# A transformer block on one Trainium2 core: the second query blocks' LayerNorm tiles turned by DMA in 16-bit halves, with three smaller moves

## The chip, the core and the metric

The kernel runs on one core of a Trainium2 chip. The core has a matrix engine (TensorE, in the profile PE, with its weight loads as PEld) and three engines for elementwise work: VectorE (DVE), ScalarE (ACT) and GpSimd (POOL). The fifth, SyncE (SP), issues nearly all DMA transfers, one after the other. Each engine works through its own instructions in order, and semaphores between the engines hold an instruction until its operands are there. TensorE writes into PSUM, of which a bank holds 128 x 512 numbers of 32 bits; everything else works from SBUF.

The metric is the device time of one execution in microseconds (us). The change is small against the whole, so differences of a few us matter, and times are given with one or two decimals.

## The reference

One block of a transformer with modulated LayerNorm: attention over the last 512 keys of a cache, then a gated feed-forward network (FFN). Cut to what matters:

```python
mod = (silu(c) @ w_mod).reshape(1, 6, 1, 512)
sa, ca, ga, sb, cb, gb = (mod[:, j] for j in range(6))
h = layernorm(x) * (1 + ca) + sa                  # x is 2048 x 512
q = (h @ wq)                                      # 32 heads of 128
p = softmax(q @ k.T * 128 ** -0.5)                # 512 keys, 8 key heads
x = x + ga * ((p @ v) @ wo)
h = layernorm(x) * (1 + cb) + sb
x = x + gb * ((gelu(h @ w_gate) * (h @ w_up)) @ w_down)     # 1792 wide
```

## The kernel before, in words

**Products in 16-bit halves.** TensorE is fed with 16-bit operands. A 32-bit number is held as two fp16 parts, a high part (a copy to fp16) and a low part (the number less its high part), and a product is made of three matmuls (`mm3`, lines 85 to 88: low x high, high x low, high x high). The first layers' products, x times wq and x times w_gate and w_up, go by a Strassen-like scheme with seven products of blocks instead of eight. Its blocks are called b11, b21, y, b22 and, for sums and differences of them, t1 to t4. They are cut from the normalised, modulated and transposed input: b11 and b21 from the first 512 queries of a half, y and b22 from the second 512.

**Stages.** The 2048 queries are worked in two halves of 1024, and each half in two query blocks (`qb`) of four tiles of 128 rows. LayerNorm therefore comes in four generations of eight tiles: generations 0 and 1 for the attention of the two halves, generations 2 and 3 for the FFN of the two halves. Attention runs as 512 steps `t`, one for each score tile (128 queries x 512 keys); a step has three score matmuls and in most steps nine others. The FFN runs as 28 sets `q` of seven products each, named (q, k); sets 0 to 13 serve the first half, 14 to 27 the second. A set has 42 matmuls, and beside the products go the output tiles `py` (`y_tasks`, six matmuls each, eight tiles for every two sets), which `y_next` places, four in a set.

**What sets the order.** In the attention part every engine's order is written out by hand: work is hung on step numbers with `at(...)`, `sched(...)` and `put_off(...)` and issued step by step, and the loads for a step wait in a list until a slot of their pool comes free. From FFN set 2 on, the program's order is fixed only for SP, while a planner that ships with the language orders TensorE, VectorE, ScalarE and GpSimd by its own estimate of when operands are ready. SP's order is the program's all the way through.

**The parts that the change touches:**

- `ln_tile` (lines 465 to 526) is the LayerNorm of a tile of generations 1 to 3: load, statistics (`ln_stat`, `ln_power`), normalisation (`norm`), four TensorE transposes of 128 x 128 in 32 bits into one PSUM bank (`turn`, line 495), the scaling by 1 + cb and shift by sb (`affine`, line 503, four ScalarE instructions of 128 x 128), and the store of the 256 KB tile to memory (`spill`, line 507). Generation 1 normalises on VectorE (line 490), generations 2 and 3 on ScalarE (lines 489 and 487). For generation 2, the tile `acc`, GpSimd makes the negative mean times the inverse deviation, `nmean` (line 482). Generation 3, the tile `xs`, finds its statistics ready, made by `ln_last` when attention ended.
- `attn_final` (line 920) hangs the seven parts of a generation 2 tile on the steps after a query tile's attention is finished: the statistics one step later, the normalisation six, the turn eight.
- Lines 1539 to 1544 hang the parts of the generation 3 tiles on products: tile i has q = 7 (2 + i // 2) + 3 (i % 2), loads at q - 4, is normalised at q + 2, turned at q + 4 and scaled at q + 5 and q + 6.
- `combos` (line 528) loads the stored blocks of a half again, makes the differences on GpSimd and their 16-bit parts on ScalarE and GpSimd (lines 363, 367 and 540). For generation 3 its two rounds start at the products numbered 49 and 63.
- The modulation rows are sums over 512 products for each output (`mod_col`, line 135: a VectorE multiply that also adds up, from a loaded tile `wmc`). Rows 3 and 4 are sb and cb. Four sums of each stand at steps 211 to 229; `mod_max` follows at 232 and `mod_scale` at 234, which turns the two maxima through TensorE and rescales both rows.
- In the profile `p<-ee,rr,p` (line 971) is the low part of the softmax, `qt` and `ot` (line 706) the low parts of queries and attention outputs, `pt<-p` (line 975) the DMA transpose of the softmax's two 16-bit halves, and `at` (line 1263) the low part of the FFN's inner result.

Of the kernel before, what the change touches and what calls it, by code (L numbers as in the profile page):

```python
# [63 lines left out]
def block_kernel(ctx: ExitStack, tc: tile.TileContext, x, kT, v, wq, wo, wg, wu, wd, cT, wc, wm, out):  # L64
# [8 lines left out]
    def tmp(name):  # L73
        return pool.tile([P, 512], F32, tag="e", name=name, bufs=NE)

    def raw(name):
        return pool.tile([P, 512], F32, tag="raw", name=name, bufs=NRAW)
# [14 lines left out]
    def dma(out_, in_):  # L92
        moved[0] += 1
        nc.sync.dma_start(out_, in_)
# [81 lines left out]
    def col(name, i=0):  # L176
        return ST[name][:, i:i + 1]
# [20 lines left out]
    def mod_max(j):  # L198
        m = little("mm", 2, 1)
        absmax(m, cols[:, j:j + 2, :])  # L200
        return m
# [34 lines left out]
    def pool_ts(out, src, a, b=1.0, op0=ALU.mult, op1=ALU.mult):  # L236
        nc.gpsimd.tensor_scalar(out, src, a, b, op0=op0, op1=op1)
# [108 lines left out]
    def spilled(gen, key):  # L346
        if (gen, key) not in hs:
            n = KT if key in (0, 1) else 2
            hs[gen, key] = dram.tile([P, n, QB], F32, name=f"hs{gen}_{key}")
        return hs[gen, key]  # L350
# [94 lines left out]
    def put_off(n, fn):  # L445

        waits_.append([n, fn])
# [17 lines left out]
    def ln_tile(gen, i, src):  # L465
        jsc, jsh = ln_cols("a" if gen < 2 else "f")
        qb, i = divmod(i % (2 * QT), QT)
        st = {}

        def load():  # L470
            if gen == 2:
                st["x"] = src()
            else:
                st["x"] = raw("xs")
                dma(st["x"], src())

        def stat():
            ln_stat(st["x"], st)
            ln_power(st)
            if gen == 2:  # L480
                st["nm"] = small.tile([P, 1], F32, name="nmean")
                pool_ts(st["nm"], st["mv"][:, 0:1], st["rs"], -1.0)

        def norm():
            if gen == 3:
                rs, nm = col("kmax", qb * QT + i), col("kinv", qb * QT + i)
                return nc.scalar.activation(st["x"], st["x"], AF.Identity, bias=nm, scale=rs)
            if gen == 2:
                return nc.scalar.activation(st["x"], st["x"], AF.Identity, bias=st["nm"], scale=st["rs"])
            nc.vector.tensor_scalar(st["x"], st["x"], st["mv"][:, 0:1], st["rs"], op0=ALU.subtract, op1=ALU.mult)  # L490

        def turn():
            st["ps"] = bank("acc", "pln", NACC)
            for dt in range(KT):
                nc.tensor.transpose(st["ps"][:, dt * P:(dt + 1) * P], st["x"][:, dt * P:(dt + 1) * P], ident)

        def affine(dts):
            if 0 in dts:
                st["f"] = raw("hf") if gen == 2 else tmp("hf")
            f = st["f"]  # L500
            for dt in dts:
                sl = slice(dt * P, (dt + 1) * P)
                nc.scalar.activation(f[:, sl], st["ps"][:, sl], AF.Identity,
                                     scale=cols[:, jsc, dt:dt + 1], bias=cols[:, jsh, dt:dt + 1])
            if KT - 1 in dts:
                def spill():
                    dma(spilled(gen, qb)[:, :, i * P:(i + 1) * P], f.rearrange("p (k q) -> p k q", k=KT))

                if gen == 3:
                    put_off(3, spill)  # L510
                else:
                    spill()

        def parts(act):
            o = slice(i * P, (i + 1) * P)
            f = st["f"].rearrange("p (k q) -> p k q", k=KT)
            for h, name in enumerate(("b11", "b21") if qb == 0 else (None, "b22")):
                if name:
                    t, src = block(gen, name), f[:, 2 * h:2 * h + 2, :]
                    if act:  # L520
                        nc.scalar.activation(t[:, 0:2, o], src, AF.Copy)
                    else:
                        nc.gpsimd.tensor_tensor(t[:, 2:4, o], src, t[:, 0:2, o], op=ALU.subtract)

        more = [lambda: parts(True), lambda: parts(False)] if gen < 3 else []
        return load, [nop if gen == 3 else stat, norm, turn, lambda: affine((0, 1)), lambda: affine((2, 3))] + more

    def combos(gen, p, eng, base=True, d=0, e=0):
        X = {}
# [167 lines left out]
    def at(key, *fns):  # L697
        later.setdefault(key, []).extend(fns)
# [425 lines left out]
    for dt in range(KT):  # L1124
        sched(6 + dt, (lambda dt=dt: gate_load(dt), [lambda dt=dt: gate_cols(dt)]), ahead=8)
    at(("d", 10), lambda: ts(cols[:, 2, :], gps["ps"][:, 0:KT], 1.0, None, ALU.mult))
    for j, ts_ in ((3, (211, 215, 223, 227)), (4, (213, 217, 225, 229)), (5, (274, 278, 282, 286))):
        for dt in range(KT):
            box = {}
            sched(ts_[dt], (lambda box=box, j=j, dt=dt: box.update(f=mod_load(j, dt)), [lambda box=box: box["f"]()]))  # L1130
    at(11, lambda: mod_row(2))
    mx = {}
    at(("w", 232), lambda: mx.update(m=mod_max(3)))
    at(234, lambda: mod_scale(3, "mf", 1.0, mx["m"]))

    def sched_combos(gen, p, base):
        for k, (load, steps) in enumerate(combos(gen, p, nc.gpsimd if gen or p == 0 else nc.vector, False, 0 if gen else 1 if p else 2, 0 if gen or p else 5)):
# [391 lines left out]
    def f_at(q, k, *fns):  # L1529
        at(("f", q, k), *fns)  # L1530
# [4 lines left out]
    for q in range(3, NQ):  # L1535
        for k, at_ in ((0, 2), (3, 2), (1, 3), (2, 4)):
            f_at(q - 1, at_, lambda q=q, k=k: set_fetch(("f", q), ("f", q % (2 * NP)), k))

    for i in range(2 * QT):
        load, steps = ln_tile(3, i, lambda i=i: y1[2 * QT + i])  # L1540
        q = 7 * (2 + i // 2) + 3 * (i % 2)
        f_at((q - 4) // 7, (q - 4) % 7, load)
        for k, fn in zip((0, 2, 4, 5, 6), steps):
            f_at((q + k) // 7, (q + k) % 7, fn)
    for p in range(2):
        q = 7 * (7 + 2 * p)
        for load, steps in combos(3, p, nc.gpsimd):
            f_at((q - 2) // 7, (q - 2) % 7, load)
            for off, fn in steps:
                f_at((q + 2 * off) // 7, (q + 2 * off) % 7, fn)  # L1550

    def f_final(ti):
        if ti >= 2 * QT:
# [6 lines left out]
    for q in range(NQ):  # L1560
        n, m = divmod(q, 2)
        its = items(NG + q) if q < 2 else f_items(q)
        for k, pk in enumerate(ORDER):
            if (q, pk) not in f_done:
                all_of(its[pk])
            run(("f", q, k))
            tick()
            if k in (1, 2, 5, 6):
                y_next()
        if m == 1:  # L1570
            for qi, (a, b) in enumerate((("11", "21"), ("12", "22"))):
                for i in range(QT):
                    nexty.append(y_tasks((2 * (n // NP) + qi) * QT + i, [lambda n=n, a=a: A[n, a], lambda n=n, b=b: A[n, b]],
                                         [("f", n, 0), ("f", n, 1)], col("dysc", n % NP), f_final if n % NP == NP - 1 else None))
# [39 lines left out]
```

## Time and profile before

| what | value |
|---|---|
| median of 3 runs | 1772.27 us (1769.34 to 1772.45) |
| the profiled execution | 1769.1 us, span 1767.3 us |
| TensorE's granted clock | 1.000 |
| TensorE / VectorE / ScalarE / GpSimd busy | 1730.0 / 1447.2 / 1219.3 / 882.2 us |
| attention's steps 0 to 511 | 26 to 1334 us of the span |
| sets 14 to 27 (second half of the FFN) | from about 1549 us |
| q1, the queue of SP's transfers | 325.44 MB, 80.0% of 16 DMA engines' span |

All times inside the kernel count from the start of the span. A row of a group has the engine, the operation, the tile written and the tiles read (`pln<-ident,xs`), partitions x elements and type, how often, and durations. Matmuls overlap: a matmul of 512 columns is shown with 0.38 us, but the next one starts 0.22 us after it, so the difference of two starts is what it costs TensorE. In a row of time order the first number is the start, the second the length, and a bracket at the end the idle time before it with what ended it. A row of waits has the waiting engine and its line, the engine and line waited for, the total, the count and the longest. A row of stretches has start and end, length, and busy time with the number of instructions in brackets for each engine, then the clock, the share of the DMA engines, and GB/s.

### The profile page before, as it was taken

Reading aid. Unit: us, or ns where it says so; the run is one execution under the profiler, and the core shown is the slowest. Engines: PE = TensorE matmul, PEld = TensorE weight load, DVE = VectorE, ACT = ScalarE, POOL = GpSimd, SP = SyncE. Lnnn points to the kernel's source line nnn. Section 1 sums busy time; section 2 is a strip of 40 time slices with the busy share of each in tenths; the row PEclk is TensorE's granted clock in tenths of the full one; section 3 lists DMA queues with packets and bytes.
Section 4 is the critical chain, followed back from the end, with each engine's and each line's share of the span. In section 5 each row is a group of like instructions: output and inputs, shape, how many; then the busy total and the mean of one; then the engine's idle time right before and its main releaser. Section 6 shows DMA issues by size and latency. Waiting matters only on the chain.

```text
span 1767.3 us, 25992 instructions
## 1 busy us (share of the span) xinstructions
PE 1730.0 (98%) x8114; PEld 796.3 (45%) x8114; DVE 1447.2 (82%) x2501; ACT 1219.3 (69%) x2830; POOL 882.2 (50%) x1119
## 2 busy tenths in 40 slices
PE   7899999999999999999999999999999999999998
PEld 4444444444444444444444444444444444444443
DVE  7888888888888998888888888888886768767676
ACT  5887787878778777897777777777674555434342
POOL 4879878776788873444565555555520024000000
PEclk9999999999999999999999999999999999999999
DMA  7999999989999997999999999999985643252222
GB/s 230 209 195 210 218 217 200 223 204 221 216 216 227 224 201 145 208 205 234 208 208 208 212 214 204 206 211 214 188 185 131 199 129 114 83 173 90 86 75 75
DMA packets 662122, 327.62 MB, mean 185 GB/s; under 512 B 553056, under 2 KB 575840, under 8 KB 661984
## 3 DMA queue, kind: packets, MB, share of 16 engines
q1 hardware_dynamic: 661696, 325.44, 80.0%
q8 instruction: 64, 1.05, 0.3%
q14 instruction: 74, 0.61, 0.1%
q10 hardware_dynamic: 288, 0.52, 0.1%
HBM read 131.73 MB, written 59.90 MB: 108 GB/s over the span
## 4 chain that ended last, share of the span: by engine, by line
PE 72%; DVE 14%; ACT 8%; issue 3%; POOL 2%; DMA 1%; SPq 0%; ACTq 0%; POOLq 0%; DVEq 0%
PE py L86 7%; PE py L88 7%; PE py L87 7%; DVE p L971 5%; PE ps L86 4%; PE ps L88 4%; PE ps L87 4%; PE po L86 4%; PE po L88 4%; PE po L87 4%; DVE nm L945 3%; PE fa L86 3%; PE fa L88 3%; PE fa L87 3%; ACT ee L954 2%
## 5 line engine op out<-in xcount | busy, mean ns | idle before, releaser
L954 ACT ACTIVATE ee<-ps,nm 128x512 f32<-128x512 f32 x512 | 350.9, 685 | 251.0 <-DVE nm L945 245.6
L971 DVE SCALAR_TENSOR_TENSOR p<-ee,rr,p 128x512 f16<-128x512 f32 x512 | 470.0, 918 | 0.9 <-ACT p L966 0.7
L945 DVE TENSOR_REDUCE nm<-ps 128x1 f32<-128x512 f32 x512 | 349.4, 683 | 77.0 <-PE ps L88 75.5
L966 ACT ACTIVATE p<-ee,rr 128x512 f16<-128x512 f32 x512 | 365.4, 714 | 2.3 <-DMA pt<-p 1.9
L86 PE MATMUL ps<-k,qt 128*128 128x512 f16 x512 | 194.1, 379 | 16.6 <-DVE qt L706 15.4
L86 PE MATMUL py<-wo,ot 128*128 128x512 f16 x512 | 194.1, 379 | 4.4 <-DVE ot L706 4.4
L87 PE MATMUL po<-pt,v 128*128 128x512 f16 x512 | 194.0, 379 | 0.0
L88 PE MATMUL po<-pt,v 128*128 128x512 f16 x512 | 194.0, 379 | 0.0
L87 PE MATMUL py<-wo,ot 128*128 128x512 f16 x512 | 194.0, 379 | 0.0
L88 PE MATMUL py<-wo,ot 128*128 128x512 f16 x512 | 194.0, 379 | 0.0
L86 PE MATMUL po<-pt,v 128*128 128x512 f16 x512 | 194.0, 379 | 0.0
L88 PE MATMUL ps<-k,qt 128*128 128x512 f16 x512 | 194.0, 379 | 0.0
L87 PE MATMUL ps<-k,qt 128*128 128x512 f16 x512 | 193.9, 379 | 0.0
L962 DVE RECIPROCAL rr<-rr 128x2 f32<-128x2 f32 x256 | 41.4, 162 | 99.6 <-ACT rr L959 98.5
L87 PEld LDWEIGHTS <-w 128*128 128x128 f16 x728 | 71.2, 98 | 86.2 <-issue 1.2
L88 PEld LDWEIGHTS <-w 128*128 128x128 f16 x728 | 71.2, 98 | 86.0 <-issue 0.2
L86 PEld LDWEIGHTS <-w 128*128 128x128 f16 x728 | 71.2, 98 | 85.5 <-DVE w L1016 0.3
L914 DVE SCALAR_TENSOR_TENSOR acc<-py,dysc,acc 128x512 f32<-128x512 f32 x112 | 81.6, 747 | 31.5 <-PE py L88 30.5
L954 ACT ACTIVATION_READ_ACCUMULATOR ee<-ps,nm 128x1 f32 x512 | 100.8, 197 | 0.0
L914 DVE SCALAR_TENSOR_TENSOR acc<-py,ysc,acc 128x512 f32<-128x512 f32 x128 | 94.7, 740 | 3.9 <-PE py L88 3.9
L706 DVE SCALAR_TENSOR_TENSOR ot<-po,ot 128x512 f16<-128x512 f32 x128 | 87.0, 680 | 0.0
L86 PE MATMUL py<-wo,at 128*128 128x512 f16 x224 | 84.9, 379 | 1.4 <-DVE at L1263 1.4
(270 smaller groups left out, 3765.9 us busy)
## 6 DMA issues: line engine op xcount, KB each, us to landing
w<-kept SPq DMA_DIRECT2D x123, 256.0 KB, 3.2
wo<-kept SPq DMA_DIRECT2D x60, 256.0 KB, 3.5
raw<-in_wo SPq DMA_DIRECT2D x56, 256.0 KB, 3.1
kept<-stage SPq DMA_DIRECT2D x56, 256.0 KB, 3.3
kept<-w SPq DMA_DIRECT2D x39, 256.0 KB, 3.4
rw<-in_wq SPq DMA_DIRECT2D x38, 256.0 KB, 3.3
hs<-hf SPq DMA_DIRECT2D x32, 256.0 KB, 2.7
pt<-p SPq DMA_TRANSPOSE x512, 3.5
```

The source lines that it names most:

```text
L86: nc.tensor.matmul(ps, llo, rhi, start=first, stop=False, skip_group_check=chain)
L87: nc.tensor.matmul(ps, lhi, rlo, start=False, stop=False, skip_group_check=chain)
L88: nc.tensor.matmul(ps, lhi, rhi, start=False, stop=last, skip_group_check=chain)
L706: return lambda: nc.vector.scalar_tensor_tensor(t[:, 1, :], src, scale, t[:, 0, :], op0=ALU.mult, op1=ALU.subtract)
L914: nc.vector.scalar_tensor_tensor(acc[ti], st["p"], by, acc[ti], op0=ALU.mult, op1=ALU.add)
L945: nc.vector.tensor_reduce(nm, E[t]["ps"], axis=AX.X, op=ALU.max, negate=True)
L954: nc.scalar.activation(e, E[t]["ps"], AF.Exp, bias=E[t]["nm"], scale=1.0, accum_out=sm[:, t % 2:t % 2 + 1])
L962: return lambda: nc.vector.reciprocal(r, r)
L966: nc.scalar.activation(p16[:, 0, :], E[t]["e"], AF.Copy, scale=E[t]["r"])
L971: nc.vector.scalar_tensor_tensor(p16[:, 1, :], E[t]["e"], E[t]["r"], p16[:, 0, :], op0=ALU.mult, op1=ALU.subtract)
```

## The change

Four things change, all in when and on which engine something is done; what is computed stays.

1. Generation 3 (the second half's input to the FFN) has a function of its own, `ln_turned`. A tile is loaded and normalised on ScalarE as before, then split into an fp16 copy (ScalarE) and its remainder (GpSimd), and both halves are turned by one DMA transpose from SP into a tile of the tag `pt`. When all four tiles of a query block are there, `turned_out` scales and shifts a whole 128 x 512 part: the high half on ScalarE, and the low half, scaled and added, on VectorE; it is stored three products later. A tile is now normalised at product q, split at q + 1 and turned at q + 3. The parts come out at products 31, 33, 35, 37 and 43 to 46, and the two rounds of `combos` start at 51 and 65.
2. Generation 2 is normalised on GpSimd, by one instruction with the mean and the inverse deviation, and `nmean` is no longer made.
3. The sums of rows 3 and 4 move from steps 211 to 229 to steps 243 to 257, `mod_max` to 258 and `mod_scale` to 260.
4. In the last set `y_next` is called after two products instead of four, so two output tiles more are left for the end.

```diff
@@ ln_tile
         def stat():
             ln_stat(st["x"], st)
             ln_power(st)
+
+        def norm():
             if gen == 2:
-                st["nm"] = small.tile([P, 1], F32, name="nmean")
-                pool_ts(st["nm"], st["mv"][:, 0:1], st["rs"], -1.0)
-
-        def norm():
-            if gen == 3:
-                rs, nm = col("kmax", qb * QT + i), col("kinv", qb * QT + i)
-                return nc.scalar.activation(st["x"], st["x"], AF.Identity, bias=nm, scale=rs)
-            if gen == 2:
-                return nc.scalar.activation(st["x"], st["x"], AF.Identity, bias=st["nm"], scale=st["rs"])
+                return pool_ts(st["x"], st["x"], st["mv"][:, 0:1], st["rs"], ALU.subtract, ALU.mult)
             nc.vector.tensor_scalar(st["x"], st["x"], st["mv"][:, 0:1], st["rs"], op0=ALU.subtract, op1=ALU.mult)
...
+    def ln_turned(i):
+
+        qb, i_ = divmod(i, QT)
+        st = {}
+
+        def load():
+            st["x"] = raw("xs")
+            dma(st["x"], y1[2 * QT + i])
+
+        def norm():
+            nc.scalar.activation(st["x"], st["x"], AF.Identity, bias=col("kinv", i), scale=col("kmax", i))
+
+        def split():
+            st["p"] = t = pool.tile([P, 2, W], F16, tag="p16", name="xh", bufs=NP16)
+            nc.scalar.activation(t[:, 0, :], st["x"], AF.Copy)
+            nc.gpsimd.tensor_tensor(t[:, 1, :], st["x"], t[:, 0, :], op=ALU.subtract)
+
+        def turn():
+            if i_ == 0:
+                TURN[qb] = pool.tile([P, QT, 2 * KT, P], F16, tag="pt", name="xt", bufs=NPT)
+            nc.sync.dma_start_transpose(TURN[qb][:, i_], st["p"].rearrange("p a b -> p (a b)"))
+
+        return load, norm, split, turn
+
+    def turned_out(qb, dt):
+        f = tmp("hf")
+        v = f.rearrange("p (t q) -> p t q", t=QT)
+        sc = cols[:, 4, dt:dt + 1]
+        nc.scalar.activation(v, TURN[qb][:, :, dt, :], AF.Identity, scale=sc, bias=cols[:, 3, dt:dt + 1])
+        nc.vector.scalar_tensor_tensor(v, TURN[qb][:, :, KT + dt, :], sc, v, op0=ALU.mult, op1=ALU.add)
+        put_off(3, lambda: dma(spilled(3, qb)[:, dt, :], f))
...
-    for j, ts_ in ((3, (211, 215, 223, 227)), (4, (213, 217, 225, 229)), (5, (274, 278, 282, 286))):
+    for j, ts_ in ((3, (243, 247, 251, 255)), (4, (245, 249, 253, 257)), (5, (274, 278, 282, 286))):
...
-    at(("w", 232), lambda: mx.update(m=mod_max(3)))
-    at(234, lambda: mod_scale(3, "mf", 1.0, mx["m"]))
+    at(("w", 258), lambda: mx.update(m=mod_max(3)))
+    at(260, lambda: mod_scale(3, "mf", 1.0, mx["m"]))
...
     for i in range(2 * QT):
-        load, steps = ln_tile(3, i, lambda i=i: y1[2 * QT + i])
         q = 7 * (2 + i // 2) + 3 * (i % 2)
-        f_at((q - 4) // 7, (q - 4) % 7, load)
-        for k, fn in zip((0, 2, 4, 5, 6), steps):
-            f_at((q + k) // 7, (q + k) % 7, fn)
+        load, norm, split, turn = ln_turned(i)
+        step(q - 4, load)
+        step(q, norm)
+        step(q + 1, split)
+        step(q + 3, turn)
+    for k, (qb, dt) in enumerate(((0, 0), (0, 2), (0, 1), (0, 3), (1, 0), (1, 2), (1, 1), (1, 3))):
+        step(31 + 2 * k if k < 4 else 39 + k, lambda qb=qb, dt=dt: turned_out(qb, dt))
     for p in range(2):
-        q = 7 * (7 + 2 * p)
+        q = 51 + 14 * p
...
-            if k in (1, 2, 5, 6):
+            if k in ((1, 2, 5, 6) if q < NQ - 1 else (1, 5)):
                 y_next()
```

More of the change, by code (lines that the diff above doesn't have):

```diff
@@ L505, in affine @@
             if KT - 1 in dts:
[L506 to L512, printed above, removed]
+                dma(spilled(gen, qb)[:, :, i * P:(i + 1) * P], f.rearrange("p (k q) -> p k q", k=KT))
         def parts(act):
@@ L523, in parts @@
                         nc.gpsimd.tensor_tensor(t[:, 2:4, o], src, t[:, 0:2, o], op=ALU.subtract)
-        more = [lambda: parts(True), lambda: parts(False)] if gen < 3 else []
-        return load, [nop if gen == 3 else stat, norm, turn, lambda: affine((0, 1)), lambda: affine((2, 3))] + more
+        more = [lambda: parts(True), lambda: parts(False)]
+        return load, [stat, norm, turn, lambda: affine((0, 1)), lambda: affine((2, 3))] + more
+    TURN = {}
+    def ln_turned(i):
[22 more added lines that the diff above has]
+        put_off(3, lambda: dma(spilled(3, qb)[:, dt, :], f))
     def combos(gen, p, eng, base=True, d=0, e=0):
@@ L1537, in block_kernel, with step @@
             f_at(q - 1, at_, lambda q=q, k=k: set_fetch(("f", q), ("f", q % (2 * NP)), k))
+    def step(q, fn):
+        f_at(q // 7, q % 7, fn)
     for i in range(2 * QT):
-        load, steps = ln_tile(3, i, lambda i=i: y1[2 * QT + i])
         q = 7 * (2 + i // 2) + 3 * (i % 2)
-        f_at((q - 4) // 7, (q - 4) % 7, load)
-        for k, fn in zip((0, 2, 4, 5, 6), steps):
-            f_at((q + k) // 7, (q + k) % 7, fn)
+        load, norm, split, turn = ln_turned(i)
[5 more added lines that the diff above has]
+        step(31 + 2 * k if k < 4 else 39 + k, lambda qb=qb, dt=dt: turned_out(qb, dt))
     for p in range(2):
-        q = 7 * (7 + 2 * p)
+        q = 51 + 14 * p
         for load, steps in combos(3, p, nc.gpsimd):
-            f_at((q - 2) // 7, (q - 2) % 7, load)
+            step(q - 2, load)
             for off, fn in steps:
-                f_at((q + 2 * off) // 7, (q + 2 * off) % 7, fn)
+                step(q + 2 * off, fn)
     def f_final(ti):
```

## The prediction

> **What bounds the kernel now.** I read the page first, then TensorE's waits, then stretches of the span.
>
> ```profile
> span 1767.3 us, 25992 instructions
> ...
> PE 1730.0 (98%) x8114; PEld 796.3 (45%) x8114; DVE 1447.2 (82%) x2501; ACT 1219.3 (69%) x2830; POOL 882.2 (50%) x1119
> ...
> PE 72%; DVE 14%; ACT 8%; issue 3%; POOL 2%; DMA 1%; SPq 0%; ACTq 0%; POOLq 0%; DVEq 0%
> ```
>
> TensorE (PE) is busy 98% of the span and is 72% of the chain that ended last. So a change counts only where it takes instructions from PE or closes one of its gaps. Its waits name the gaps:
>
> ```profile
> PE ps L86 <- DVE qt L706: 15.4, 12, 2.7
> ...
> PE py L86 <- DVE ot L706: 4.4, 4, 1.7
> ...
> PE pln L495 <- ACT hf L503: 1.5, 2, 0.8
> PE py L86 <- DVE at L1263: 1.4, 1, 1.4
> ```
>
> Each is total, count, longest. Most is PE waiting for VectorE (DVE). The stretches that the change touches, busy microseconds by engine:
>
> ```profile
> core 0: us, PE busy (x) PEld busy (x) DVE busy (x) ACT busy (x) POOL busy (x), PEclk, DMA share, GB/s
> 525.00:565.00 40.00, 39.40 (x187) 17.84 (x186) 34.76 (x59) 32.55 (x79) 34.30 (x43) 1.00 0.92 212
> 565.00:635.00 70.00, 66.13 (x307) 29.39 (x305) 65.90 (x125) 49.02 (x120) 59.62 (x71) 1.00 0.95 218
> 650.00:690.00 40.00, 38.25 (x179) 17.18 (x177) 33.47 (x55) 28.52 (x68) 20.44 (x22) 1.00 0.80 154
> 690.00:800.00 110.00, 107.46 (x515) 50.65 (x514) 93.61 (x177) 93.27 (x229) 47.00 (x63) 1.00 0.90 197
> 1375.00:1450.00 75.00, 75.00 (x365) 36.21 (x364) 50.16 (x77) 43.82 (x84) 2.80 (x8) 1.00 0.53 165
> 1450.00:1550.00 100.00, 100.00 (x465) 45.32 (x464) 75.71 (x109) 47.57 (x78) 27.89 (x21) 1.00 0.30 100
> ```
>
> From 1375 to 1550, where the second query blocks' LayerNorm tiles are now turned, PE never rests while ACT, DVE and GpSimd (POOL) do: work leaving PE there is gained whole. From 565 to 635, where eight modulation sums run, PE loses 3.87 and DVE is 94% busy. From 690 to 800, where the first blocks are normalised, PE loses 2.54.
>
> **Part A, the turns.** One turn as PE sees it:
>
> ```profile
> L495 PE MATMUL pln<-ident,xs x32: 272/273/273, 1385.3 to 1435.4; 128*128 128x128 f32 x32
> ```
>
> ```profile
> 1385.13 0.38 PE L88 MATMUL fc<-t,w 128*128 128x512 f16 x1
> 1385.35 0.60 PE L495 MATMUL pln<-ident,xs 128*128 128x128 f32 x4
> 1385.78 0.38 PE L86 MATMUL fa<-b,w 128*128 128x512 f16 x1
> ```
>
> The next product starts 0.43 us after the first of four transposes; the 273 ns are length, not pace. Eight tiles: 8 x 0.43 = 3.4 us leave a PE that has no gap. What comes instead, by the nearest rows (copies to 16 bit, their remainders, DMA transposes, a DVE multiply-add):
>
> ```profile
> L363 ACT ACTIVATE t<-cb x8: 614/629/631, 1452.1 to 1485.7; 128x512 f16<-128x512 f32 x8
> L367 POOL TENSOR_TENSOR t<-cb,t x8: 1151/1598/1613, 1454.6 to 1487.2; 128x512 f16<-128x512 f32 x8
> ```
>
> ```profile
> L975 SPq DMA_TRANSPOSE pt<-p x16: 1231/1232/1318, 656.5 to 692.7; - x16
> ```
>
> ```profile
> pt<-p SPq DMA_TRANSPOSE x512, 3.5
> ```
>
> ```profile
> 601.41 1.62 DVE L135 SCALAR_TENSOR_TENSOR wmc<-wmc,sbc 128x512 f32<-128x512 f32 x1
> ...
> 603.63 1.65 DVE L971 SCALAR_TENSOR_TENSOR p<-ee,rr,p 128x512 f16<-128x512 f32 x1
> ...
> 618.59 0.68 DVE L135 SCALAR_TENSOR_TENSOR wmc<-wmc,sbc 128x512 f32<-128x512 f32 x1
> ```
>
> ACT keeps eight normalisations, loses 32 quarter-size scalings, gains eight copies (0.63) and eight full-size scalings; POOL gains 8 x 1.6 = 12.8; DVE 8 x 0.68 = 5.4 (8 x 1.62 = 13.0 beside POOL); loads and stores stay eight of 256 KB each. All of it lies under PE: of the 175 us, DVE is idle 49, ACT 84, POOL 144. I take nothing; without that cover the DVE part alone would cost 5.4. The chain's end moves by two steps: the last remainder starts at 1487.2, and the second half's first products start here:
>
> ```profile
> 1549.85 0.38 PE L86 MATMUL fa<-b,w 128*128 128x512 f16 x1
> ```
>
> That leaves about 61 us; a set has 66 matmuls at 0.216 us, so two steps of its seven are some 4 us. The new wait is on SP, whose order is the program's: eight transposes of 1.23 us stand there behind POOL's remainder, and behind them the next tiles' loads and the next sets' weights. Before, the tile's store waited there in the same way:
>
> ```profile
> SPq L94 <- ACT hf L503: 18.4, 2, 16.5
> ```
>
> ```profile
> 1407.30 0.58 SPq L94 DMA_DIRECT2D w<-kept  x1
> ```
>
> ```profile
> w<-kept SPq DMA_DIRECT2D x31, 256.0 KB, 3.5
> ```
>
> ```profile
> 1411.70 0.38 PE L86 MATMUL fa<-b,w 128*128 128x512 f16 x1
> ```
>
> One store held SP 16.5 us and PE still did not wait; the tightest fetch I find lands at 1410.8 and is used 0.9 us later. The new chain skips PE's turn, so SP should wait less: nothing, with up to 8 x 2.6 (below) as the other end. Part A: -3.4, between -3.4 and +17.
>
> The Trainium skill speaks against this part: "VectorE: DVE Perf Modes", section "Rules for kernel authors", would give a 128x128 transpose to TensorE wherever a PSUM result will do, and its section "The three transpose paths" has 390 ns there against 1309 ns by DMA. By its figures, an estimate, 64 half-tiles by DMA are 84 us against 12.5 for 32 on TensorE. Were none of it hidden, part A would lose some 70 us by the page, where the rows give -3.4. The trace differs on both figures: 0.11 us of pace here, and 3.5 us for eight half-tiles by DMA.
>
> **Part B, the sums for the shift and scale of the second LayerNorm** move from steps 211-229 to 243-257, their scaling from 234 to 260: from the stretch 565-635 to 650-695. A step has three score matmuls, and counted in order those of step 243 begin here:
>
> ```profile
> 650.93 0.38 PE L86 MATMUL ps<-k,qt 128*128 128x512 f16 x1
> ```
>
> ```profile
> 565.00:635.00 70.00, 8.66 (x16) 1.00 0.95 218
> ```
>
> ```profile
> DVE nm L945 <- PE ps L88: 5.4, 7, 1.2
> ```
>
> ```profile
> L971 DVE SCALAR_TENSOR_TENSOR p<-ee,rr,p x17: 731/741/1257, 655.3 to 694.5; 128x512 f16<-128x512 f32 x17
> ```
>
> The sums take 8.66 of DVE in the old place (first row). The 40 us before them, like work without sums, lose 0.60, so 70 us would lose 1.05: the gain is 3.87 - 1.05 = 2.8. In the new place POOL is half idle, so I price a sum at 0.68 and its read-out 0.08, together 8 x 0.76 = 6.1, against 6.5 of idle DVE, 5.4 of which is DVE waiting for PE (second row, 655 to 695). What doesn't fit is 6.1 - 5.4 = 0.7. The eight loads leave a stretch with DMA share 0.95 for one with 0.80. Part B: -2.1, between -3.9 (all of the old gap goes) and +3.3 (all 6.1 is lost, 2.8 gained).
>
> **Part C, the first blocks' normalisation goes from ACT to POOL.**
>
> ```profile
> 741.06 0.81 ACT L489 ACTIVATE acc<-acc,nmean,rs 128x512 f32<-128x512 f32 x1
> 741.76 0.68 ACT L954 ACTIVATE ee<-ps,nm 128x512 f32<-128x512 f32 x1
> ...
> 743.61 0.81 ACT L503 ACTIVATE hf<-pln,cols 128x128 f32<-128x128 f32 x2
> ```
>
> ```profile
> 744.48 0.66 PE L495 MATMUL pln<-ident,acc 128*128 128x128 f32 x4 [0.79 <-ACT hf L503]
> ```
>
> ```profile
> L237 POOL TENSOR_SCALAR gs<-gate,osc x8: 683/692/1123, 68.9 to 588.4; 128x512 f32<-128x512 f32 x8
> ```
>
> A turn waits until ACT has read the bank before it; ACT spent 0.7 us just ahead (741.06 to 741.76) on the normalisation. Two such waits make the 1.5 of the list: without it both shrink by 0.7, -1.4. POOL pays 8 x 0.69 and drops eight small products; it is busy 47 of 110, and the normalisation comes two steps of twelve matmuls, some 5 us, ahead of its turn. Ends: -2.5 (all idle time of the stretch) and +6.7: beside POOL the DVE row of p took 1.65 where 0.74 is its median in the quiet stretch, some 0.84 more for each of eight. I take -1.4, since the wait is seen and DVE has 16 us to spare.
>
> **Part D, two of the last pair's output tiles wait for the end.**
>
> ```profile
> 1755.58 0.39 PE L86 MATMUL py<-wo,at 128*128 128x512 f16 x1 [1.39 <-DVE at L1263]
> ```
>
> At the end PE has nothing ready for 1.39 us. Two tiles of six matmuls (2.6 us) now lie there: -1.4. Their two accumulations could push DVE's last halves by 2 x 0.68, so the end on the other side is 0.
>
> **Sum.** -3.4 - 2.1 - 1.4 - 1.4 = -8.3. The profiled execution took 1769.1, 1.8 more than its span; the median of the runs, 1772.27, lies 3.2 above it. From the median: 1764.0; from the profiled execution 1760.8.
>
> **Rivals.** *The gaps only move* (0.20). B and C give nothing, since DVE stays at nine tenths and some other step waits: 1772.3 - 3.4 - 1.4 = 1767.5. For it: DVE holds most of PE's waits; against it: its 5.4 idle us in the new place.
>
> *The sums crowd DVE* (0.12). B costs its 3.3, C nothing: 1772.3 - 3.4 + 3.3 - 1.4 = 1770.8. For it: a gap of 1.75 stands in 650-690 already. The rows of one DVE instruction at 0.68 and 1.62 are what decides.
> The Trainium skill's "SBUF — State Buffer", section "SBUF: two separate sides", says why: DVE with two SBUF inputs and POOL lock one port pair, and the later blocks. The trace agrees (0.68 against 1.62).
>
> *SP's queue starves PE* (0.10), the slower side. Each transpose holds SP for copy, remainder and issue, 0.63 + 1.60 + 1.23 = 3.5; less the 0.9 of slack, weights could come 2.6 late, eight times: 1764.0 + 20.5 = 1784.5. It decides from 1.5 us a turn (8.3 + 3.5 over eight). Against it: 16.5 us cost nothing before.
>
> *The detour by DMA is late for the second half* (0.01). It needs 57 us more than the rows give; from there each microsecond counts whole, so from 8.3 + 3.5 beyond it the kernel is slower: 1775.8. This is the side of the skill's rule above.
>
> **How the numbers follow.** The forecast has 0.57. About 0.2%, 3.5 us, is what a measurement tells from no change. Forecast and first rival are faster by more: 0.77; the second is the same: 0.12; the last two slower: 0.11. The low end takes the best of B and C: -3.4 - 3.9 - 2.5 - 1.4 = -11.2 from 1769.1, 1757.9, put at 1757; the high end, 1771, takes in the second rival.
>
> **What would show it.** No PE transposes after 1350 and no gap there; the gaps between 565 and 635 down to about 1 us; PE's idle time in 650-690 under 2.5; no wait of pln for hf; no 1.39 at the end. A PE wait for weights between 1380 and 1450, or new waits for qt at 650-690, would make me wrong.

## The result, and the profile after

The changed kernel takes 1765.4 us (median of 6 runs, 1761.96 to 1765.8) against 1772.4 us (6 runs, 1769.34 to 1773.13) for the kernel before: a ratio of 0.9958, with a 95% interval of 0.9946 to 0.9971. It is 7.0 us faster, where 8.3 was forecast. The profiled execution took 1765.8 us. From its page:

```profile
span 1764.0 us, 25952 instructions
...
PE 1731.7 (98%) x8082; PEld 793.8 (45%) x8082; DVE 1451.4 (82%) x2509; ACT 1213.7 (69%) x2806; POOL 902.4 (51%) x1127
```

PE has 32 instructions fewer, the transposes. What TensorE waits for in the changed kernel (total, count, longest):

```profile
PE ps L86 <- DVE qt L728: 12.8, 12, 2.8
...
PE fa L86 <- ACT fg L869: 2.2, 2, 1.6
PE pln L489 <- POOL acc L237: 2.2, 2, 1.1
PE py L86 <- DVE ot L728: 1.6, 2, 0.9
PE fa L86 <- DMA w<-kept: 1.6, 2, 0.9
...
PE py L86 <- DVE at L1285: 0.2, 1, 0.2
```

The wait for `ot` has gone from 4.4 to 1.6 and the last one from 1.4 to 0.2. The wait of `pln` for ScalarE is gone, but one of 2.2 for GpSimd's `acc` stands in its place. Two others are of `fa`, a product of the FFN: for a PSUM bank that ScalarE has yet to read (2.2, 0.7 of which before had too), and for fetched weights (1.6, new). The stretches of the prediction, same columns, in the changed kernel:

```profile
565.00:635.00 70.00, 69.37 (x325) 31.21 (x323) 60.05 (x106) 53.40 (x132) 60.65 (x75) 1.00 0.96 210
650.00:690.00 40.00, 39.37 (x184) 17.64 (x182) 39.15 (x77) 28.04 (x67) 19.77 (x21) 1.00 0.94 194
690.00:800.00 110.00, 107.48 (x516) 50.67 (x515) 98.08 (x184) 87.73 (x218) 61.67 (x65) 1.00 0.91 201
1375.00:1450.00 75.00, 74.26 (x344) 33.45 (x343) 58.00 (x86) 43.62 (x68) 10.67 (x11) 1.00 0.61 172
1450.00:1550.00 100.00, 97.54 (x452) 43.96 (x450) 74.56 (x107) 47.10 (x77) 29.99 (x22) 1.00 0.35 111
```

TensorE's idle time (length less its first number) falls from 3.87 to 0.63 in 565-635 and from 1.75 to 0.63 in 650-690. It stays at 2.5 in 690-800, and from 1375 to 1550 it rises from nothing to 3.2.

Fixed stretches slide against the work, so I also timed the work itself. A score step has three products `ps<-k,qt`, and counting them gives the start of each step. This table has the time from one step to another in microseconds, in the profiled execution of each kernel; the last column runs to the end of the span. The runs e1 to e12 are described below.

| kernel | 0-50 | 200-229 | 229-257 | 257-300 | 511-end |
|---|---|---|---|---|---|
| before | 128.92 | 76.94 | 74.35 | 114.59 | 433.09 |
| after | 131.82 | 73.93 | 72.03 | 114.85 | 432.28 |
| e1, part A alone | 130.99 | 77.14 | 73.78 | 114.63 | 432.35 |
| e2, part B alone | 131.83 | 73.95 | 72.03 | 114.85 | 433.95 |
| e3, part C alone | 130.98 | 77.38 | 74.40 | 114.07 | 433.67 |
| e4, part D alone | 130.99 | 76.67 | 74.12 | 114.62 | 434.21 |
| e5, without part C | 131.15 | 73.53 | 72.04 | 115.01 | 432.39 |
| e6, sums' work again | 131.01 | 75.18 | 72.04 | 114.33 | 432.79 |
| e7, sums' loads again | 131.13 | 73.95 | 72.03 | 114.65 | 432.29 |
| e10, sums twice | 128.90 | 76.81 | 72.57 | 114.82 | 430.93 |
| e11, GpSimd in two | 128.91 | 73.52 | 72.03 | 117.48 | 432.04 |
| e8, stores later | 129.87 | 74.10 | 72.04 | 114.63 | 431.58 |
| e9, read-back later too | 129.90 | 73.21 | 72.03 | 114.60 | 428.11 |
| e12, and a scaled add | 128.93 | 73.81 | 72.03 | 114.98 | 428.50 |

From before to after: 200-257 gives 5.3 (part B; the four kernels with the sums in the old place alone take 150.8 to 151.8 us there, the seven with them in the new place alone 145.2 to 146.1). The end gives 0.8 (part A; the four kernels with the old turns take 433.1 to 434.2, those with part A and its read-back as in after 430.9 to 432.8, so one pair of profiles says little about 1 us). 257-300 costs 0.3, and it does so in e2 too, with part B alone. The first column has nothing to do with the change: it runs from 128.9 to 131.8 in kernels that are alike there (last section). The profiled execution of before had a short one, 2.9 us less than after, which is the larger part of why the two profiles differ by 3.3 us where the medians differ by 7.0.

### The profile page after: what moved, and what is told of

Read it like the earlier page. It is cut to its first block, busy times and chain, and to the rows that moved or that the text cites. A ratio compares the mean times of both kernels' runs of the same rounds, so it can differ in the third digit from the quotient of the medians.

```text
span 1764.0 us, 25952 instructions
## 1 busy us (share of the span) xinstructions
PE 1731.7 (98%) x8082; PEld 793.8 (45%) x8082; DVE 1451.4 (82%) x2509; ACT 1213.7 (69%) x2806; POOL 902.4 (51%) x1127
## 4 chain that ended last, share of the span: by engine, by line
PE 67%; DVE 16%; ACT 9%; issue 4%; POOL 3%; DMA 2%; SPq 0%; POOLq 0%; DVEq 0%; ACTq 0%
PE py L86 7%; PE py L88 7%; PE py L87 7%; DVE p L993 5%; PE ps L86 4%; PE ps L88 4%; PE ps L87 4%; PE po L86 4%; PE po L88 4%; PE po L87 4%; DVE nm L967 3%; PE fa L86 2%; PE fa L88 2%; PE fa L87 2%; ACT ee L976 2%
```

## The experiments

**One part at a time.** Four kernels, each the kernel before with one part of the change, timed on one chip beside the kernel before (1771.75 us, median of 30 runs).

Run e1, part A alone: `ln_turned`, `turned_out` and their places, nothing else.

> The kernel before with the turns by DMA alone (part A). My theory after the two traces: the 3.4 us that TensorE saves are given back between 1430 and 1485, where the trace after shows new TensorE gaps of 3.8 us in sum, because SP holds the next weights behind the stores of the turned tiles; so this kernel is within 1 us of the kernel before. The rival, the prediction's own term: 3.4 us faster, with no new gap, and the gaps in the trace after come from another part.

Measured: 1770.4 us (11 runs), ratio 0.9988 (0.9980 to 0.9997). TensorE's waits in e1:

```profile
PE fa L86 <- ACT fg L872: 2.2, 2, 1.5
PE fa L86 <- DMA w<-kept: 1.6, 2, 1.0
...
PE py L86 <- DVE at L1288: 0.5, 1, 0.5
```

Part A brings its own waits of `fa`, and it shortens the last wait without part D. Its gain by the ratio is 2.1 us (0.5 to 3.5), and 0.7 by the table's last column. That interval holds a gain of under 1 us as well as one of 3.4; it is the new waits that speak for the theory.

Run e2, part B alone:

```diff
-    for j, ts_ in ((3, (211, 215, 223, 227)), (4, (213, 217, 225, 229)), ...
+    for j, ts_ in ((3, (243, 247, 251, 255)), (4, (245, 249, 253, 257)), ...
-    at(("w", 232), lambda: mx.update(m=mod_max(3)))
-    at(234, lambda: mod_scale(3, "mf", 1.0, mx["m"]))
+    at(("w", 258), lambda: mx.update(m=mod_max(3)))
+    at(260, lambda: mod_scale(3, "mf", 1.0, mx["m"]))
```

> The kernel before with the modulation sums moved alone (part B). My theory: this is the larger part of the gain, 4 to 5 us, since TensorE's idle time between steps 200 and 300 falls and none comes back in the new place. The rival, the prediction's term: 2.1 us, with 0.7 us lost in the new place.

Measured: 1767.1 us (8 runs), ratio 0.9973 (0.9963 to 0.9983). By the ratio part B gains 4.8 us (3.0 to 6.6) and is the largest part. Its stretch 565-635 comes out as in the changed kernel:

```profile
565.00:635.00 70.00, 69.29 (x324) 31.19 (x323) 60.00 (x107) 53.36 (x132) 60.75 (x74) 1.00 0.97 209
```

Run e3, part C alone:

```diff
-                return nc.scalar.activation(st["x"], st["x"], AF.Identity, bias=st["nm"], scale=st["rs"])
+                return pool_ts(st["x"], st["x"], st["mv"][:, 0:1], st["rs"], ALU.subtract, ALU.mult)
```

The three lines that made `nmean` are out as well.

> The kernel before with the first blocks' normalisation on GpSimd alone (part C). My theory: within 0.5 us of the kernel before, the turn's wait for ScalarE (1.5 us) gone and a wait for GpSimd of about the same size in its place. The rival, the prediction's term: 1.4 us faster.

Measured: 1771.2 us (11 runs), ratio 0.9995 (0.9986 to 1.0004): no difference that can be told. A row of the groups in e3:

```profile
L237 POOL TENSOR_SCALAR acc<-acc,mv,rs 128x512 f32<-128x512 f32 x8 | 17.7, 2208 | 0.0
```

A normalisation takes 2.2 us on the mean on GpSimd (the median is 2.08), not the 0.69 of the row that I had priced it by, and TensorE waits 2.2 us for it at two turns, as in the changed kernel.

Run e4, part D alone:

```diff
-            if k in (1, 2, 5, 6):
+            if k in ((1, 2, 5, 6) if q < NQ - 1 else (1, 5)):
```

> The kernel before with two output tiles left for the end alone (part D). Both my theory and the prediction: the last wait of TensorE falls from 1.39 us to about 0.2 and the time by 1.2 to 1.4 us. The rival: the wait moves to the next late result and the time stays.

Measured: 1771.4 us (11 runs), ratio 1.0001 (0.9992 to 1.0009): nothing. The last wait of TensorE stands as before:

```profile
PE py L86 <- DVE at L1263: 1.4, 1, 1.4
```

In the FFN the order of TensorE's instructions is not the program's: a planner puts them in order. In before and in e4 alike, 36 matmuls `py` come after the last `fc`; with part A (e1 and after) there are 39, and 46 in e8 and e9 below, where no wait is left at the end. So the gain at the end came with part A's plan, not with part D.

**Part C beside the rest.** Run e5 is the changed kernel with ScalarE's normalisation and `nmean` put back (the edit of e3, reversed). This run and e6 to e8 stood beside the kernel before at 1771.2 us (11 runs).

> The changed kernel with part C alone undone: the first blocks' normalisation is on ScalarE again, with its nmean on GpSimd. Theory (from the trace after: a normalisation on GpSimd lasts 2.2 us on the mean, not the 0.69 that I took, and TensorE waits for it 2.2 us at two turns, where it waited 1.5 for ScalarE before): part C is worth no more than 0.6 us, so the time is 1765 to 1766 us; the wait of pln for acc on GpSimd goes and a wait of pln for hf on ScalarE of about 1.5 comes back. Rival (the prediction's term): part C is worth 1.4, so the time is about 1766.8 us. Second rival: the POOL normalisation costs more than it saves beside the other parts, and the time is 1764.5 us or less.

Measured: 1764.1 us (5 runs), ratio 0.9964 (0.9951 to 0.9976). The median lies where the second rival puts it, but the ratio does not differ from that with part C (0.9958, 0.9946 to 0.9971), so the runs don't tell whether part C costs anything. The wait of `pln` for ScalarE is back (1.7 us) and the one for GpSimd gone. Part C exchanges one for the other.

**What made the old gap at 565-635.** Three kernels put parts of the old sums back, beside the moved ones that give the result. Run e6 has the work without loads (a maximum of the row with itself leaves the row as it is):

```diff
+    def spin():
+        nc.vector.scalar_tensor_tensor(sbc, sbc, 1.0, sbc, op0=ALU.mult, op1=ALU.max, accum_out=col("gam", 1))
+
+    for t in (211, 213, 215, 217, 223, 225, 227, 229):
+        at(("w", t), spin)
```

> The changed kernel with eight extra VectorE multiply-adds of the sums' shape at the steps where the sums stood before (211 to 229), without loads: each takes the broadcast row with itself and leaves it as it is, and its sum goes to a place that is written again before it is read. Theory (VectorE's time in 565-635 made the old gap): TensorE's idle time from 565 to 635 us rises from 0.63 to 2.5 to 4 us, and the time by 2 to 4 us, to about 1768 us. Rival (it was the loads, or the raw slots that they held, or the place of the loads in the queue): idle time stays at about 0.6 and the time at 1765.4 us.

Measured: 1765.8 us (7 runs), ratio 0.9971 (0.9960 to 0.9981). Run e7 has the loads without the work:

```diff
+    for t, j, dt in ((211, 3, 0), (213, 4, 0), (215, 3, 1), (217, 4, 1), (223, 3, 2), (225, 4, 2), (227, 3, 3), (229, 4, 3)):
+        sched(t, (lambda j=j, dt=dt: mod_load(j, dt), [nop]))
```

> The changed kernel with eight extra loads of 256 KB into the raw slots at the steps where the sums stood before, without VectorE's work on them. Theory: the old gap was VectorE's time, so TensorE's idle time from 565 to 635 us stays under 1 us and the time within 0.7 us of the changed kernel's 1765.4 us. Rival: the loads and their slots made the gap, or the part of the gain of 4.6 us that VectorE's time does not explain (about 1.8): idle time of 2 us or more there or behind it, and a time of 1767 us or more.

Measured: 1763.4 us (5 runs), ratio 0.9956 (0.9942 to 0.9970). Run e10, beside the kernel before at 1771.4 us, has both: the loads of e7, each with this step in place of none

```diff
+        return lambda: nc.vector.scalar_tensor_tensor(t, t, 1.0, sbc, op0=ALU.mult, op1=ALU.mult, accum_out=col("gam", 1))
```

> The changed kernel with the eight sums made a second time at their old steps (211 to 229), with their own loads, each on the row that it loaded; the sum itself is thrown away. The two runs that put back the work alone and the loads alone gave 1.5 us and nothing in TensorE's idle time from 565 to 635 us, where the kernel before lost 3.2 us more than the changed one. Theory (the two act together: a sum that stands in VectorE's order with the row it waits for): idle time of 565-635 rises from 0.63 to 3 to 4 us, and the time by 3 to 4.6 us, to 1768.5 to 1770 us. Rival (the work alone is all, and the rest of the old gap came from the scaling at step 234 or from chance in the order): 2 to 2.5 us idle there, as with the work alone, and about 1767 us.

Measured: 1765.2 us (5 runs), ratio 0.9964 (0.9951 to 0.9976). The stretch 565-635 of e6, e7 and e10, in this order:

```profile
565.00:635.00 70.00, 67.87 (x317) 30.50 (x316) 65.36 (x121) 52.51 (x129) 64.12 (x74) 1.00 0.93 202
```

```profile
565.00:635.00 70.00, 69.22 (x324) 31.19 (x322) 59.91 (x108) 53.72 (x132) 57.65 (x72) 1.00 1.05 230
```

```profile
565.00:635.00 70.00, 67.15 (x312) 29.86 (x311) 65.04 (x120) 51.38 (x127) 60.48 (x71) 1.00 1.00 225
```

Idle: 2.13, 0.78 and 2.85, against 0.63 without any and 3.87 in before; e6 and e10 stay somewhat below what was expected of them, and e7's time is 1.3 us below its range. By the steps 200-229, where the moved parts have no share, the work alone costs 1.3 of the 3.0 us, the loads alone nothing, both together 2.9. So nearly all of the old loss is the sums, and a little under half of it is VectorE's time alone. How the loads add to it the rows don't show: VectorE waits 0.2 us for a loaded row in e10. One place of the loss in before: the sum at 601.41 took 1.62 us and the `p` behind it 1.65 (rows of the prediction), and behind those, in the time order of VectorE, stood

```profile
605.21 0.68 DVE L706 SCALAR_TENSOR_TENSOR ot<-po,ot 128x512 f16<-128x512 f32 x1
```

whose end TensorE's longest wait for `ot`, 1.7 us, awaited. The totals of e6 and e10 missed what was expected (about 1768, and 1768.5 to 1770): in e10 the steps 200-229 lost what they should, and other stretches were shorter than in after (the last one by 1.4, whose plan is made anew for each kernel, and the first by 2.9). For differences of this size the steps tell more than the total.

**What holds part A back.** SP's waits in the changed kernel from 1375 to 1490:

```profile
SPq L94 <- PE fa L88: 30.5, 6, 11.9
SPq L94 <- DVE hf L547: 23.6, 6, 7.0
SPq L538 <- POOL xh L533: 3.2, 3, 2.0
```

At the turns (line 538) SP waits 3.2 us in all. At the stores of the turned tiles it waits 23.6, with the next loads and weights behind them. The chain of waits of the changed kernel goes through two of these stores:

```profile
1418.70 0.32 SPq L94
...
1419.43 1.24 SPq L538
...
1420.73 3.15 DMA xs<-y
1423.90 0.82 ACT xs L528
...
1427.39 0.76 DVE hf L547
1428.17 0.32 SPq L94
...
1429.01 4.00 DMA w<-kept
1433.05 0.39 PE fa L86
```

```profile
1448.09 0.76 DVE hf L547
1448.87 0.32 SPq L94
...
1449.74 5.55 DMA cb<-hs
...
1464.10 1.27 POOL cb L562
...
1468.70 1.57 DVE fg L1282
...
1470.84 0.59 ACT fg L869
1471.47 0.38 PE fa L86
```

First: a store, behind it a turn and a tile's load, whose normalisation delays the next `hf`, whose store delays a load of weights, for which TensorE waits. Second: the last store, right behind it the read-back (`combos`), and its copies stand in the orders of GpSimd, ScalarE and VectorE ahead of the work that frees TensorE's bank. Between two starts of products the three gaps cost 0.90 (1433), 1.07 (1459) and 1.72 us (1471) more than the usual 0.22, 3.7 in all.

Run e8 puts the stores off longer, and the read-back behind them:

```diff
-        put_off(3, lambda: dma(spilled(3, qb)[:, dt, :], f))
+        put_off(6, lambda: dma(spilled(3, qb)[:, dt, :], f))
-        q = 51 + 14 * p
+        q = 54 + 14 * p
```

> The changed kernel with the eight stores of the turned tiles put off six steps in place of three, and the work that reads them back three steps later. Theory (SyncE stands at these stores waiting for VectorE, up to 7.0 us each, and the next sets' weights behind them come late): SyncE's wait for hf falls from 23.6 us to under 8, TensorE's waits for the fetched weights (0.9 us at 1433 and 1.07 us at 1459) go, and the time falls by 1 to 2 us, to about 1764 us. Rival (the gaps come from the order in which the planner now puts TensorE's, ScalarE's and VectorE's work): other gaps of the same size come in their place and the time stays at 1765.4 us. In both the 1.7 us wait for a bank that ScalarE reads may stay, since the store has no part in it.

Measured: 1764.4 us (5 runs), ratio 0.9963 (0.9951 to 0.9976), no different from after's. The gaps for weights at 1433 and 1459 are gone, as the first theory has it, but SP still waits 22.3 us for `hf`, and gaps of 1.7 and 1.4 us stand at 1467 and 1471, as the rival has it. Its chain there:

```profile
1449.45 0.32 SPq L94
1449.82 4.94 DMA cb<-hs
...
1469.30 1.57 DVE at L1285
1470.91 0.39 PE py L86
```

The first of these rows is a load of weights, issued 1.1 us after the last store (1448.35); the read-back, `cb`, still comes right behind, and its copies stand in this chain as in the one before. Run e9 moves the read-back away (`q = 68 + 14 * p`, the rest as e8); it and e11 stood beside the kernel before at 1771.4 us.

> The run with the stores put off six steps, and the work that reads them back (combos of the third LayerNorm, on GpSimd and ScalarE) another 14 steps later, some 29 us. In that run two gaps of 1.7 and 1.4 us stand at 1467 and 1471 us, where VectorE's multiply-adds take 1.4 to 1.75 us beside GpSimd instead of 0.69. Theory (the gaps come from that overlap): no gap of 1 us or more from 1455 to 1485 us; what comes later is 2 us or less, and the time falls by 1 to 2 us, to about 1763 us. Rival (the gaps come from the planner's order of TensorE's products around there): a gap of 1 us or more stays between 1455 and 1480 us, and the time stays at 1764.4 us.

Measured: **1758.7 us** (5 runs, 1758.13 to 1761.52), ratio 0.9931 (0.9919 to 0.9944), the fastest kernel of the study and faster than was expected. By the ratio it is faster than both after and e8. Not all of that is the read-back: of the 7.0 us between the spans of after and e9, 4.2 lie behind step 511, 1.9 in the first column and 0.7 in steps 200-229, where e9 has nothing of its own. Against e8 the last column falls by 3.5. Two stretches, and a group of VectorE's from 1450 to 1530:

```profile
1375.00:1450.00 75.00, 75.00 (x349) 34.03 (x348) 58.87 (x90) 45.27 (x72) 9.89 (x8) 1.00 0.65 175
1450.00:1550.00 100.00, 100.00 (x465) 45.22 (x463) 77.98 (x106) 47.45 (x78) 32.23 (x22) 1.00 0.32 102
```

```profile
L1282 DVE SCALAR_TENSOR_TENSOR fg<-fg,u 128x512 f32<-128x512 f32 x6 | 6.6, 1101 | 0.1
```

TensorE does not rest from 1375 to 1550, and its chain there is its own products alone. The slow VectorE instructions are still there (1.1 us on the mean in this group, 0.88 in the changed kernel), so the overlap with GpSimd, which I had named as the cause, is not enough for a gap. SP's wait for `hf` is hardly less either: 21.4 us in e9 from 1375 to 1490. So what costs time is not the wait but what stands behind it. What e9 changes against e8 is the place of the read-back alone, and with it the planner's order; this run can't separate the two.

**What GpSimd's normalisation costs.** Run e11 is the changed kernel with two instructions in place of one:

```diff
-                return pool_ts(st["x"], st["x"], st["mv"][:, 0:1], st["rs"], ALU.subtract, ALU.mult)
+                pool_ts(st["x"], st["x"], st["mv"][:, 0:1], 1.0, ALU.subtract, ALU.mult)
+                return pool_ts(st["x"], st["x"], st["rs"])
```

> The changed kernel with GpSimd's normalisation in two instructions, one subtracts the mean and one multiplies by the reciprocal deviation, each with one operand by partition and the constant 1 beside it. Theory (2.08 us is the price of the form with two operands by partition, and a form with one takes the 0.69 of my row): two instructions of about 0.7 us each, 1.4 in all; the waits of TensorE for acc fall from 2.2 us to 1 or less, and the time by up to 1 us, to 1764.5 us. Rival (the price comes from what runs beside it, or from the subtraction): the two together take 2 us or more, the waits stay at about 2.2 and the time at 1765.4 us.

Measured: 1765.7 us (7 runs), ratio 0.9968 (0.9957 to 0.9979). The two groups (min/median/max in ns):

```profile
L237 POOL TENSOR_SCALAR acc<-acc,mv x8: 1991/2002/2505, 704.6 to 780.2; 128x512 f32<-128x512 f32 x8
L237 POOL TENSOR_SCALAR acc<-acc,rs x8: 694/698/1203, 706.7 to 782.3; 128x512 f32<-128x512 f32 x8
```

The rival holds: it is the instruction with the subtraction, 2.00 us, where the one that multiplies takes 0.70 (both then multiply by 1). Run e12 is e9 with a form without subtraction, `nmean` made as before the change:

```diff
-                return pool_ts(st["x"], st["x"], st["mv"][:, 0:1], st["rs"], ALU.subtract, ALU.mult)
+                return pool_ts(st["x"], st["x"], st["rs"], st["nm"], ALU.mult, ALU.add)
```

> The run with the stores six steps off and the read-back 14 steps later (1758.7 us, where TensorE waits 2.2 us for acc on GpSimd), with GpSimd's normalisation as one multiplication by the reciprocal deviation and one addition of the mean times it (nmean), in one instruction. Theory (the run with two instructions showed 2.00 us for the one that subtracts and 0.70 for the one that multiplies; subtraction alone is dear): the instruction takes about 0.7 us, TensorE's waits for acc on GpSimd fall from 2.2 us to 0.7 or less, and the time is 1756.5 to 1758 us. Rival (any sum with an operand by partition is dear there): it takes 2 us, the waits stay at about 2, and the time is 1758 to 1759.5 us.

Measured: 1760.7 us (5 runs, 1759.03 to 1762.01) beside the kernel before at 1771.2, ratio 0.9943 (0.9930 to 0.9957), which does not differ from e9; the 1756.5 to 1758 of the theory are missed.

```profile
L237 POOL TENSOR_SCALAR acc<-acc,rs,nmean x8: 757/764/1267, 704.9 to 778.4; 128x512 f32<-128x512 f32 x8
```

The instruction does take 0.76 us, and TensorE's wait for `acc` falls from 2.2 to 0.7. But from 690 to 800 it now waits 0.9 for ScalarE at a turn and 1.2 for VectorE's `ot`, and steps 257-300 take as long as ever (115.0). That stretch does not hang on the normalisation.

## Why the prediction was right

The time came out at 1765.4 for a forecast of 1764.0, the sum at 7.0 for 8.3. The terms did not: one was much too small, and three too large. That the total came so close is luck: what part B gave beyond its term made up for more than half of what the other three did not give.

*Part A, "-3.4", and "nothing" for SP.* The transposes left PE as priced, and the last wait fell by 1.2 with the new plan. Against these 4.6 stand 3.7 us of new gaps. What is left, 0.9, is what the table shows within 0.1 (433.1 to 432.3). The step that failed is "the new chain skips PE's turn, so SP should wait less": I followed the queue to the turns and not to the new stores, which wait for the end of a longer chain, ScalarE and then VectorE, in an order that the planner sets later than SP's order assumes. The rival "SP's queue starves PE" happened in part, at the stores: 0.9 + 1.07 for weights, and 1.72 for the read-back that follows. The wait for weights at 1433 is one that the prediction had named beforehand as a sign of being wrong, as it had a gap behind 1350. "All of it lies under PE" failed with it: average idle time of ScalarE, VectorE and GpSimd did not keep a dependent chain from ending late. With the stores later and the read-back moved away (e9) the last column falls by 5.0 from before: the transposes' 3.4 and the last wait's 1.4 make nearly all of it. So the price of the transposes was right, and the work that replaced them can be hidden, but not where the change put it. The rule of the Trainium skill against this part ("VectorE: DVE Perf Modes", section "Rules for kernel authors") would keep such transposes on TensorE; here DMA was the better place, as e9 shows, where SP waits 2.6 us in all at the eight turns and TensorE does not rest.

*Part B, "-2.1".* It was 5.1 by the table (5.3 gained in 200-257, 0.3 lost behind), and 4.8 by the ratio of e2. Two steps were mis-sized. The old place lost 3.0 rather than 2.8, which is good; but the new place was to lose 0.7 and lost nothing. VectorE is busy 39.15 of 40 us in 650-690, and TensorE's idle time fell there, from 1.75 to 0.63. "What doesn't fit is 6.1 - 5.4" counted only the time in which VectorE waited for TensorE as free. The remaining 2.3 lie in steps 229-257, and their cause stays open. In before TensorE loses 0.7 us there at 621.97 and 1.9 at 654.14, in after 0.8 at 651.12; but e1, whose sums stand in the old place too, loses only 1.1 at the second. In e10, where the sums run in both places, 1.8 of the 2.3 stay gained; they may have come with moving the scaling from step 234, to which I had given no price, but that was not tried by itself.

*Part C, "-1.4".* It is nothing (e3, e5, e12). The step that failed is "POOL pays 8 x 0.69": the row that I took multiplies, and this one subtracts, 2.08 us in the changed kernel. The wait moved from ScalarE to GpSimd. Even at the price that I had taken (e12) nothing is gained, since other waits take its place: the rival "the gaps only move" holds for this part, and not for part B.

*Part D, "-1.4".* Alone it did nothing (e4): the planner leaves as many `py` for the end as before, 36, whatever the program's order says. The gain at the end is there, under part A.

*The base.* The forecast was set against the median, 3.2 above the profiled execution. That was right, though the prediction gave no reason for it: the profiled execution of before lacked a loss at the start that every profile of e1 to e4 has (128.9 against 131.0 to 131.8 in the first column).

## What to carry to other kernels

Price what a change adds to a queue at each instruction that waits, the stores as well as the loads, and ask what stands behind it: here a store that waits for two engines held up the weights, and with the read-back behind the last store that cost as much as the transposes saved, until both were put later. Take a duration from a row with the same arithmetic, not only with the same engine, instruction, shape and type. And where a part's gain is a few microseconds, time the work between two marks of its own in several traces: parts that cancel give a right total for wrong reasons.

## What was not expected of the hardware

**Subtraction on GpSimd.** For 128x512 in 32 bits, with operands by partition: subtract the operand 2.00 us, subtract it and multiply 2.08, multiply 0.70, multiply and add 0.76 (e11, after, e12). The subtracted operand is always the mean; that this operand itself is dear to read is not what the rows suggest, since `kinv<-mv,rs`, a multiplication of 128x1 that reads it, takes 0.26 us like others of that size. The Trainium skill, "GPSIMD Engine Reference", section "4.1 Engine selection", calls operations with one tensor input roughly line-rate there. The runs don't show that rate itself, but a subtraction that takes three times as long as a multiplication can't be at the same one.

**A wait of some 2 us can halve TensorE's pace.** In e11 one wait was longer than in the changed kernel:

```profile
740.96 1.11 PE L490 MATMUL pln<-ident,acc 128*128 128x128 f32 x4 [2.15 <-POOL acc L237]
741.86 0.63 PE L86 MATMUL ps<-k,qt 128*128 128x512 f16 x1
742.29 0.63 PE L87 MATMUL ps<-k,qt 128*128 128x512 f16 x1
...
744.42 0.38 PE L86 MATMUL po<-pt,v 128*128 128x512 f16 x1
```

Behind it six products start 0.43 us apart instead of 0.22, 1.3 us lost beside the wait, and the four transposes ahead of them take 0.90 instead of 0.43; steps 257-300 of e11 took 117.5. The same happens, or not, at the waits of the start. The stretch 60-78 of before and of the changed kernel, with the granted clock third from the end:

```profile
60.00:78.00 18.00, 14.28 (x68) 6.22 (x66) 15.00 (x28) 15.65 (x39) 12.94 (x20) 1.00 0.90 202
```

```profile
60.00:78.00 18.00, 14.94 (x65) 6.27 (x64) 14.98 (x29) 14.50 (x36) 12.80 (x20) 0.91 0.89 191
```

Both have a gap of 2.7 us near 67, and only one lost its clock. This is the first column of the table: profiles with no such slow stretch take 128.9 us for steps 0 to 50, with one 129.9 (e8, e9), with two 131.0 to 131.2, with three 131.8 (e2, after). The Trainium skill, "TensorE: Matmul & The Clock Gate", section "What's actually happening", has the clock halved after an idle window of about 3.4 us that runs freely of the work. That it depends on where the gap falls agrees with these rows; that it takes 3.4 us does not, since 2.15 was enough in e11, and in after 1.69 us at 25.5, with two shorter waits (0.52 and 0.36) in the 5 us ahead of it.
